# A two-layer decode step with its gradients: first MLP's products ahead of its turnings, three early zero pieces, three of K's groups loaded a second time

## The chip, the cores and the metric

The kernel is one program on one core of a Trainium2 chip. The metric is the device time of one execution in microseconds (us). The core has five engines that run beside each other and wait for each other by semaphores: TensorE (PE in the profile; its weight loads are PEld), VectorE (DVE), ScalarE (ACT), GpSimd (POOL) and SyncE (SP, which here only starts transfers). 16 DMA engines move data between the chip's memory (HBM) and the on-chip memory (SBUF); TensorE writes to PSUM, which has 8 banks.

## The reference

One token passes through attention (A), an MLP (B), the same attention and the same MLP again, with the same weights both times. Then the gradients of the output with regard to the input, both caches and all weights are returned.

```python
def _A_ref(x, k_cache, v_cache, wq, wo):          # x [1,1,1024]; caches [1,4,32768,128]
    W = min(4096, max(256, Sk // 4))              # 4096: only the last 4096 keys count
    q = (x @ wq).reshape(B, Sq, Hq, Dh)           # 32 heads of 128, 4 groups of keys
    k = jnp.repeat(k_cache[:, :, Sk - W:, :], rep, axis=1)
    v = jnp.repeat(v_cache[:, :, Sk - W:, :], rep, axis=1)
    p = _softmax(jnp.einsum("bhqd,bhkd->bhqk", q, k) * (Dh ** -0.5), axis=-1)
    return (p @ v).reshape(...) @ wo              # wo [4096,1024]
def _B_ref(x, w1, b1, w2):                        # w1 [1024,3584], w2 [3584,1024]
    h = x @ w1 + b1
    return (h * jnp.tanh(softplus(h))) @ w2
x = x + _A_ref(_layernorm(x), ...)
x = x + _B_ref(_layernorm(x), ...)
x = x + _A_ref(_layernorm(x), ...)
x = x + _B_ref(_layernorm(x), ...)
_out, _vjp = jax.vjp(_f, A_x, A_k_cache, A_v_cache, A_wq, A_wo, B_w1, B_b1, B_w2)
return (_out, *_vjp(grad_out))
```

All data are bf16. The gradients of the two caches are as large as the caches (4 x 32768 x 128 each), and zero outside the last 4096 keys: 56 MB of zeros have to be written. (MB here and below, where sizes of tiles and pieces are told, is 1024 x 1024 bytes.)

## The kernel before

**Stages in order.** Attention of layer 0, MLP of layer 0 ("first MLP"), attention and MLP of layer 1, then backward: MLP of layer 1 (its first part is done in the forward pass, below), attention of layer 1, MLP of layer 0, attention of layer 0, and at the end the outer products that make the weight and cache gradients (the "wide" stage, which takes PSUM in tiles of 1024 columns, named `wide`), evacuated to SBUF and stored. The order is written out by hand: the program has no scheduler, and each engine does its instructions in the order of the code.

**Weights and slots.** All loads go through one queue, SP's. `Ring` (the class at the top) holds a list of wanted transfers and eight slots of 1 MB; `pump` starts the next wanted transfer as soon as a slot is free, and `release` frees a slot and pumps. Its order is K, queries of layer 0, V, two chunks of w2 (`EARLY_2`), wo, w1, the other five chunks of w2 (chunk 3 goes to `zt`, the tile that later holds zeros), then three chunks of wq for layer 1 (five stay in the ring from layer 0, `KEEP_Q`), wo, wq, w2, wo and wq for what follows. A slot is freed where its last reader stands in the code, so what stands early in the code of a stage sets when the next load starts.

**Zeros.** `zeros(n, after)` (line 259 to 264) writes n pieces of 1 MB of zeros out of `zt`, by DMAs from POOL's queue; with `after`, POOL first copies one element of a tile, and so waits until that tile is computed. There are 56 such pieces. `zt` is set to zero (line 728) after the first MLP, which uses it for chunk 3 of w2.

**Products with one vector.** A product of a weight matrix with a vector uses the matrix as TensorE's stationary operand, 128 x 128 at a time, and has one moving column. The backward products need the matrix transposed: `turned` (line 446) transposes eight blocks on TensorE into a PSUM bank (line 450, the "turning"), `evac` copies them back over the matrix (line 303 on DVE, line 306 on ACT), and `mv` (line 462) does the product. `later` holds products back so that TensorE does other work while a copy runs; `flush` does all that are held back. Alternatively `rowdot` (line 427) does such a product on DVE, row by row. `rows_chunk` splits a chunk of four rows between the two.

**First MLP** (lines 716 to 738). w2 comes in seven chunks. For each, `mlp_out` (line 673) multiplies with the activation `AC` for the forward result; and since the gradient that arrives at the very end is an input, the same chunk is used at once for the backward product of layer 1's MLP, the `da` values: two rows on DVE, two turned. Chunks 0 and 1 had their `da` done earlier on DVE. `last_da` does chunk 6 as the first thing of the next stage, through `q_hook`, called once after the layer norm of layer 1's attention; it ends the collection of `da1`.

**K and V.** K is loaded in natural order into `W1S`, turned into `KT` by `kt_transposes` (line 587), and used so by the scores of both layers. V is used as it comes, in `VS`. The backward products need K in natural order and V turned, so all 32 units of eight blocks (`conv_units`, 16 of K, 16 of V) are turned in place, on TensorE (line 602) with a copy on ACT or DVE. `conv(n, eng)` does the next n units; `conv_pe` and `conv_ev` do the two halves. Units are placed where other work waits: one after the scores, one beside the softmax, one after each of eight chunks of the output projection (`wo_hook1`), eight after layer 1's MLP (line 767, beside `deriv`), and two for each chunk of the backward output projection of layer 1 (`do` hook) until none is left.

**Backward.** `dn_b1` does w1's backward product of layer 1, `ln_bwd` the layer norm's, whose hook `beside` is called twice around a small product on TensorE. `attn_bwd` has its own hooks: `do` after each of eight wo chunks, `dp`, `dq`, and `dn` after each of eight wq chunks. In layer 0 the `dn1` hook writes zero pieces at t = 3, 6 and 7, and `units_a0` (as `beside`) starts the final stage's units.

## Time and profile before

| what | value |
|---|---|
| median of 3 runs (lowest to highest) | 460.42 us (459.21 to 463.47) |
| the profiled execution's own time | 461.23 us |
| its span, first to last instruction | 459.2 us |
| TensorE / its weight loads / DVE / ACT / POOL busy | 341.7 / 276.6 / 256.6 / 225.0 / 38.7 us |
| bytes moved by DMA, mean rate | 179.38 MB, 391 GB/s (MB and GB of ten) |
| of it on SP's queue (q1), on POOL's (q0), for instructions (q8) | 119.74, 58.72, 0.80 MB |
| mean granted TensorE clock | 0.629 |

Some places in the profiled execution, in us from the start of the span: the first MLP's products start at 90.35 and its result is there at 105.45 (DVE, line 385); the queries of layer 1 are ready at 120.40; layer 1's attention result at 150.49; the gradient enters the backward attention of layer 1 at 191.31 and of layer 0 at 298.05 (DVE, line 846); the wide stage starts at 353.85 (TensorE, line 1015); the last computing instruction ends at about 437, and SP issues the last store at about 448.

How to read it: the page of the profile has the busy times, then the span in 40 slices of 11.48 us with one digit of busy share each, the granted TensorE clock and the DMA rate; then queues; then the chain of work that ended last; then groups of equal instructions by line. A line can be that of a helper (306 is every copy on ACT). The trace answers more: instructions in order of time on one engine, with the idle time before and what ended it in brackets, and the busy time of every engine in a chosen stretch (columns: length, then PE, PEld, DVE, ACT and POOL busy with counts, granted clock, DMA share, GB/s).

### The profile page before, as it was taken

What the parts mean: (1) busy time and instruction counts of PE and PEld (TensorE: products, weight loads), DVE (VectorE), ACT (ScalarE), POOL (GpSimd) and SP (SyncE); (2) the same over time, 40 slices, a digit from 0 to 9 for tenths busy, and PEclk for the clock granted to TensorE, in tenths of its full rate; (3) what the DMA queues carried; (4) which work ended last, traced back from release to release, by engine and by line L of the source; (5) the groups of instructions that cost most, each with busy time, mean ns of one, the idle gap of its engine ahead of it and who ended that gap; (6) DMA issues with size and microseconds to landing.
All of it is one profiled execution on the core that took longest, in us unless ns stands there. A gap on an engine that the chain in (4) does not pass through costs nothing. (4 is left out here: it accounts for less than half of the span.)

```text
span 459.2 us, 14200 instructions
## 1 busy us (share of the span) xinstructions
PE 341.7 (74%) x6361; PEld 276.6 (60%) x6361; DVE 256.6 (56%) x516; ACT 225.0 (49%) x261; POOL 38.7 (8%) x85
## 2 busy tenths in 40 slices
PE   3836445598679888598879798798797888889900
PEld 3735434497569887498779798697693222224600
DVE  4505731283060149677528676657456999998810
ACT  2502001055045379377317555157064999999900
POOL 1000000030103322200211000101221000000000
PEclk9955555555555569699759955589586555555555
DMA  8999999877999999999999988999999999999995
GB/s 337 421 420 418 418 419 416 361 278 261 385 425 422 421 417 418 415 399 415 420 422 418 421 320 298 347 344 368 422 419 424 412 422 422 418 421 416 405 407 213
DMA packets 27802, 179.38 MB, mean 391 GB/s; under 512 B 3642, under 2 KB 3670, under 8 KB 9430
## 3 DMA queue, kind: packets, MB, share of 16 engines
q1 hardware_dynamic: 19586, 119.74, 65.5%
q0 software_dynamic: 8064, 58.72, 30.9%
q8 instruction: 49, 0.80, 0.6%
q14 instruction: 11, 0.09, 0.0%
q10 hardware_dynamic: 92, 0.02, 0.0%
HBM read 79.74 MB, written 98.62 MB: 388 GB/s over the span
## 5 line engine op out<-in xcount | busy, mean ns | idle before, releaser
L306 ACT COPY ring<-BIG 128x1024 bf16<-128x1024 bf16 x62 | 60.7, 1014 | 41.5 <-PE BIG L450 36.1
L450 PE MATMUL BIG<-ident_bf,ring 128*128 128x128 bf16 x744 | 67.4, 255 | 1.8 <-ACT W L306 1.1
L450 PEld LDWEIGHTS <-ring 128*128 128x128 bf16 x816 | 61.5, 116 | 2.8 <-issue 2.2
L1015 PE MATMUL wide<-W 2*128 2x512 bf16 x228 | 52.1, 598 | 9.3 <-ACT W L306 2.0
L427 DVE CUSTOM_DVE_ANT_0 junk<-ring,SC 128x1024 bf16<-128x1024 bf16 x34 | 41.3, 1215 | 5.4 <-DMA ring<-in_B_w_dram 3.7
L1015 PEld LDWEIGHTS <-W 2*128 2x128 bf16 x240 | 12.6, 102 | 44.3 <-issue 43.2
L462 PEld LDWEIGHTS <-ring 128*128 128x128 bf16 x912 | 31.6, 98 | 9.3 <-ACT ring L306 6.7
L306 ACT COPY KT<-BIG 128x1024 bf16<-128x1024 bf16 x22 | 21.8, 1016 | 30.3 <-PE BIG L602 28.7
L303 DVE CAST ring<-wide 128x1024 bf16<-128x1024 f32 (+1 forms) x29 | 33.7, 1199 | 3.2 <-PE wide L1015 1.5
L306 ACT COPY W<-BIG 128x1024 bf16<-128x1024 bf16 x28 | 26.7, 1119 | 16.0 <-PE BIG L788 14.9
L306 ACT CAST ring<-wide 128x1024 bf16<-128x1024 f32 (+1 forms) x35 | 32.9, 1018 | 1.3 <-PE wide L1066 0.5
L303 DVE COPY ring<-BIG 128x1024 bf16<-128x1024 bf16 x31 | 21.3, 690 | 19.3 <-PE BIG L450 12.2
L264 POOL DMA_DIRECT2D out_dram<-zt x56 | 29.7, 534 | 22.9 <-DMA out_dram<-zt 22.0
L621 PE MATMUL MV<-NB,W 128*128 128x1 bf16 x448 | 16.2, 172 | 9.3 <-DMA W<-in_B_w_dram 6.5
L493 PE MATMUL MV<-NA,ring 128*128 128x1 bf16 x512 | 14.9, 165 | 11.0 <-DMA ring<-in_A_wq_dram 8.6
L621 PEld LDWEIGHTS <-W 128*128 128x128 bf16 x448 | 15.9, 118 | 9.8 <-DMA W<-in_B_w_dram 7.2
L303 DVE CAST VS<-wide 128x1024 bf16<-128x1024 f32 (+1 forms) x17 | 19.7, 1186 | 3.6 <-PE wide L1015 3.0
L1066 PE MATMUL wide<-W 32*128 32x256 bf16 x128 | 20.9, 402 | 0.9 <-ACT ring L306 0.8
L306 ACT CAST KT<-wide 128x1024 bf16<-128x1024 f32 x20 | 20.4, 1032 | 1.8 <-PE wide L1015 0.9
L493 PEld LDWEIGHTS <-ring 128*128 128x128 bf16 x512 | 14.2, 103 | 11.5 <-DMA ring<-in_A_wq_dram 9.1
L427 DVE CUSTOM_DVE_ANT_0 junk<-ring,DSX 128x1024 bf16<-128x1024 bf16 x16 | 19.6, 1224 | 1.1 <-DMA ring<-in_B_w_dram 0.7
L427 DVE CUSTOM_DVE_ANT_0 junk<-W,SC 128x512 bf16<-128x512 bf16 (+1 forms) x20 | 15.8, 791 | 6.5 <-PE SC L330 5.8
(268 smaller groups left out, 566.9 us busy)
## 6 DMA issues: line engine op xcount, KB each, us to landing
out_dram<-zt POOLq DMA_DIRECT2D x56, 1024.0 KB, 16.2
ring<-in_A_wq_dram SPq DMA_DIRECT2D x22, 1024.0 KB
ring<-in_A_wo_dram SPq DMA_DIRECT2D x14, 1024.0 KB
ring<-in_B_w_dram SPq DMA_DIRECT2D x13, 1024.0 KB
W<-in_A_wo_dram SPq DMA_DIRECT2D x10, 1024.0 KB
W<-in_B_w_dram SPq DMA_DIRECT2D x8, 896.0 KB
out_dram<-ring SPq DMA_DIRECT2D x7, 1024.0 KB
out_dram<-ring SPq DMA_DIRECT2D x13, 512.0 KB
```

Source lines behind the costliest of these rows:

```text
L264: nc.gpsimd.dma_start(dst, zt[:])
L303: nc.vector.tensor_copy(dst, src)
L306: nc.scalar.copy(dst, src)
L427: nc.vector.tensor_tensor_reduce(out=out, in0=a, in1=vec, scale=1.0, scalar=acc if i else 0.0, op0=ALU.mult, op1=ALU.add, accum_out=acc)
L450: nc.tensor.transpose(b[:, i * P:(i + 1) * P], block(w, i) if block else w[:, i * P:(i + 1) * P], ident_bf[:])
L462: nc.tensor.matmul(out, lhsT=w[:, i * P:(i + 1) * P], rhs=rhs_of(i), start=fresh[0], stop=last and i == n - 1, skip_group_check=True)
L493: nc.tensor.matmul(q_ps[:, h:h + 1], lhsT=ch[:, h * P:(h + 1) * P], rhs=NA[:, t, l:l + 1], start=(k == 0 and h == 0), stop=(k == TD - 1), ...
L621: nc.tensor.matmul(h_ps[:, fb:fb + 1], lhsT=f_block(W1[:, t], fb), rhs=NB[:, t, l:l + 1], start=(t == 0 and fb == 0), stop=(t == TD - 1), ...
L1015: nc.tensor.matmul(b[:, 512 * i:512 * i + 512], lhsT=R[at:at + 2, lo:lo + P], rhs=R[at:at + 2, ro + 512 * i:ro + 512 * i + 512], start=Tru ...
L1066: nc.tensor.matmul(b[:, k * 256:(k + 1) * 256], lhsT=RT[32 * g:32 * g + 32, a, tp, :], rhs=YS[32 * g:32 * g + 32, :], start=True, stop=Tru ...
```

## The change

Five edits stand in one diff.

1. First MLP: `turned` is cut into `turn_pe` and `turn_ev`, and the loop over chunks is written out. Chunk 2's turning stands first, then the forward products of chunks 0, 1, 2 and 3, with turnings, copies, DVE's rows and the products of the turned rows between and behind them. Chunks 5 and 6 are turned in the next stage: `q_hook` is now called with -1 where it was called before, and with k after each of the eight query chunks, and `last_da` does its parts at -1, 1 and 3. A chunk is released after its turned rows' products (`da_mv`).
2. Three zero pieces are written right after `zt` is set to zero; the hook `dn1` writes one piece instead of four in all.
3. `K_TURNED = 1`: only K's group 0 is turned back. Groups 1, 2 and 3 are loaded a second time from the cache into `KT`, by three transfers of 1 MB on SP's queue that stand behind the last product with `KT` in layer 1's scores. 20 units are left.
4. The 20 units stand elsewhere: one after the scores, two beside the softmax, one behind the softmax's sum, two in the output projection (chunks 2 and 5), one before the MLP's first product, four after the MLP, three and one around `ln_bwd` in `dn_b1`, five in the backward output projection (chunks 1 to 5).
5. `beside` gets the number of its call.

```diff
--- before.py
+++ after.py
@@ -402,10 +402,10 @@
         nc.vector.scalar_tensor_tensor(out=t2[:], in0=dn[:], scalar=1.0, in1=n32[:], op0=ALU.mult, op1=ALU.mult,
                                        accum_out=st[:, 1:2])
         if beside is not None:
-            beside()
+            beside(0)
         nc.tensor.matmul(TP[:, 128:130], lhsT=onesD[:], rhs=st[:], start=True, stop=True)
         if beside is not None:
-            beside()
+            beside(1)
         ab = tmp([P, 2], FP32, "ab")
         nc.vector.tensor_copy(ab[:], TP[:, 128:130])
         nc.vector.scalar_tensor_tensor(out=t2[:], in0=n32[:], scalar=ab[:, 1:2], in1=dn[:], op0=ALU.mult,
@@ -443,12 +443,19 @@
         while lag:
             lag.popleft()[1]()
 
-    def turned(w, n, mv, eng=None, block=None):
+    def turn_pe(w, n, block=None):
 
         b = big().bitcast(BF16)
         for i in range(n):
             nc.tensor.transpose(b[:, i * P:(i + 1) * P], block(w, i) if block else w[:, i * P:(i + 1) * P], ident_bf[:])
+        return b
+
+    def turn_ev(w, b, n, eng=None):
         evac(w, b[:, 0:n * P], eng, cost=(0.69 * n / 8, n / 8))
+
+    def turned(w, n, mv, eng=None, block=None):
+
+        turn_ev(w, turn_pe(w, n, block), n, eng)
         later(mv, True)
 
     fresh = [False]
@@ -484,7 +491,7 @@
         if first:
             kt_transposes()
         if q_hook is not None:
-            q_hook()
+            q_hook(-1)
         q_ps = MV[:, 0:HQ]
         order = list(range(TD)) if l == 0 else sorted(range(TD), key=lambda t: t not in KEEP_Q)
         for k, t in enumerate(order):
@@ -496,6 +503,8 @@
                 ring.keep(("q", 0, t), ("q", 1, t))
             else:
                 ring.release(("q", l, t))
+            if q_hook is not None:
+                q_hook(k)
         qv = QC[:].rearrange("p v (g u l h) -> p v g u l h", g=G, u=2, l=2)
         nc.vector.tensor_scalar(out=qv[:, 0, :, 0, l, :], in0=q_ps.rearrange("p (g h) -> p g h", g=G), scalar1=scale,
                                 scalar2=None, op0=ALU.mult)
@@ -512,6 +521,8 @@
             nc.vector.reduce_max(m64[i][:], SC[i].rearrange("p (tp c) -> p c tp", c=64), axis=AX.X)
         if not first:
             conv(1, "A")
+            for g in range(K_TURNED, G):
+                nc.sync.dma_start(KT[:, g], kv_src(A_k_cache, g))
         nc.vector.tensor_tensor(out=m64[0][:], in0=m64[0][:], in1=m64[1][:], op=ALU.max)
         m32 = small[:, 128:160]
         m64v = m64[0][:].rearrange("p (g u h) -> p g u h", g=G, u=2)
@@ -527,7 +538,7 @@
         nm = small[:, 224:288]
         nc.vector.tensor_copy(nm[:], TP[:, 192:256])
         if not first:
-            late = conv_pe(1)
+            late = conv_pe(2)
         for i in range(2):
             s = SC[i].rearrange("p (tp c) -> p tp c", c=64)
             nc.vector.tensor_tensor(out=s, in0=s, in1=nm[:, None, :].to_broadcast([P, 8, 64]), op=ALU.subtract)
@@ -550,6 +561,8 @@
         for u in range(2):
             nc.tensor.matmul(TP[:, 256:288], lhsT=onesD[:], rhs=ssv[:, :, u, :], start=(u == 0), stop=(u == 1))
 
+        if not first:
+            conv(1, "A")
         rs = small[:, 288:320]
         nc.vector.tensor_scalar(out=rs[:], in0=TP[:, 256:288], scalar1=float(D), scalar2=None, op0=ALU.mult)
         nc.vector.reciprocal(rs[:], rs[:])
@@ -588,7 +601,8 @@
                 evac(KT[:, g, 8 * b8:8 * b8 + 8, :], b.rearrange("p (t s) -> p t s", t=8))
             ring.release(("K", g))
 
-    conv_units = [(KT, g, b8) for g in range(G) for b8 in range(4)] + [(VS, g, b8) for g in range(G) for b8 in range(4)]
+    K_TURNED = 1
+    conv_units = [(KT, g, b8) for g in range(K_TURNED) for b8 in range(4)] + [(VS, g, b8) for g in range(G) for b8 in range(4)]
     conv_units.reverse()
 
     def conv_pe(n):
@@ -615,6 +629,8 @@
     def mlp_fwd(l, x, st):
         name = f"B{l}"
         n32, rstd = ln_fwd(x, st, NB[:, :, l], name)
+        if l:
+            conv(1, "A")
         h_ps = MV[:, 192:192 + TF]
         for t in range(TD):
             for fb in range(TF):
@@ -716,31 +732,76 @@
     mp0 = sB0["deriv"]()
     y_ps = MV[:, 256:256 + TD]
     mv_open()
-    for c in range(7):
+    held = {}
+
+    def da_out(c):
+        mlp_out(0, ring.get(("2", 0, c)), c, y_ps)
+
+    def da_dots(c):
         ch = ring.get(("2", 0, c))
-        mlp_out(0, ch, c, y_ps)
-        flush()
+        for tt in range(2):
+            rowdot(ch[:, tt, :], [gbc], D, da1[:, 4 * c + tt:4 * c + tt + 1])
+
+    def da_turn(c):
+        ch = ring.get(("2", 0, c))
+        held[c] = [(ch[:, tt, :], turn_pe(ch[:, tt, :], TD)) for tt in (2, 3)]
+
+    def da_put(c):
+        for w, b in held[c]:
+            turn_ev(w, b, TD, "A")
+
+    def da_mv(c):
+        for tt, (w, _) in zip((2, 3), held.pop(c)):
+            r = DA + 4 * c + tt
+            mv(w, TD, TP[:, r:r + 1], lambda i: GB[:, i, 1:2], True)
+        ring.release(("2", 0, c))
+
+    da_turn(2)
+    for c in range(3):
+        da_out(c)
         if c in EARLY_2:
             ring.release(("2", 0, c))
-        elif c < 6:
-            rows_chunk(ch, c, GB, 1, gbc, da1, DA)
-            later(lambda c=c: ring.release(("2", 0, c)))
+    da_put(2)
+    da_dots(2)
+    da_out(3)
+    da_turn(3)
+    da_put(3)
+    da_dots(3)
+    da_mv(2)
+    da_out(4)
+    da_mv(3)
     nc.gpsimd.memset(zt[:], 0.0)
+    zeros(3)
+    da_turn(4)
+    da_put(4)
+    da_dots(4)
+    da_out(5)
+    da_dots(5)
+    da_mv(4)
+    da_out(6)
     x2, st2 = residual(y_ps, x1, "B0")
 
 
-    def last_da():
-
-        rows_chunk(ring.get(("2", 0, 6)), 6, GB, 1, gbc, da1, DA)
-        flush()
-        ring.release(("2", 0, 6))
-        v = da1[:, 8:TF].rearrange("p (a b) -> p a b", b=4)[:, :, 2:4]
-        nc.vector.tensor_copy(v, TP[:, DA + 8:DA + TF].rearrange("p (a b) -> p a b", b=4)[:, :, 2:4])
+    def last_da(k):
+
+        if k == -1:
+            da_turn(5)
+            da_put(5)
+            da_dots(6)
+        elif k == 1:
+            da_mv(5)
+            da_turn(6)
+            da_put(6)
+        elif k == 3:
+            da_mv(6)
+            v = da1[:, 8:TF].rearrange("p (a b) -> p a b", b=4)[:, :, 2:4]
+            nc.vector.tensor_copy(v, TP[:, DA + 8:DA + TF].rearrange("p (a b) -> p a b", b=4)[:, :, 2:4])
 
     def wo_hook1(c):
         if c == 0:
             zeros(7, OC[:, 0, 1:2])
-        conv(1)
+        if c in (2, 5):
+            conv(1)
 
     DR = {}
     stg = DSX[0:2 * HQ, 1024:1024 + 4 * P].rearrange("p (k i) -> p k i", k=4)
@@ -764,7 +825,7 @@
     zeros(8, x3)
     sB1 = mlp_fwd(1, x3, st3)
     put_by("NB", NB, TD)
-    conv(8, "A")
+    conv(4, "A")
     mp1 = sB1["deriv"]()
 
 
@@ -800,7 +861,8 @@
                 turned(w, n, lambda w=w, f0=f0, n=n, t=t, k=k: mv(w, n, TP[:, t:t + 1], lambda i: DHC[:, f0 + i, 1:2], k == 1),
                        "A", f_block)
         flush()
-        return ln_bwd(dnp, sB1["n32"], sB1["rstd"], g, "B1")
+        conv(3, "A")
+        return ln_bwd(dnp, sB1["n32"], sB1["rstd"], g, "B1", lambda k: conv(k, "A"))
 
     def rowize_f():
 
@@ -952,7 +1014,7 @@
             zeros(1, dnp[:, t:t + 1])
 
     g2 = attn_bwd(1, sA1, g3, ("o", 1), ("q", 2), KEEP_Q2,
-                  dict(do=lambda c: conv(2), dp=dp3, dq=dq3, dn=dn3))
+                  dict(do=lambda c: conv(1 if 1 <= c <= 5 else 0), dp=dp3, dq=dq3, dn=dn3))
 
 
     ROWS = W1S[:, 0:5120]
@@ -1142,14 +1204,14 @@
         zeros(4, DQC[:, 0, 0:1])
 
     def dn1(t):
-        if t in (3, 6, 7):
-            zeros(2 if t == 3 else 1, dnp[:, t:t + 1])
+        if t == 3:
+            zeros(1, dnp[:, t:t + 1])
         if t == 4:
             twins()
         if t == 5:
             todo[0].append(units_cols(0, 8, out_4))
 
-    def units_a0():
+    def units_a0(k):
 
         even()
         load["D"] += 10
```

## The prediction

> **What bounds the kernel now.** I read the page's slices first, then the DMA queues, then stretches around the two dips, and last POOL's own order of work. The slices:
>
> ```profile
> DMA  8999999877999999999999988999999999999995
> GB/s 337 421 420 418 418 419 416 361 278 261 385 425 422 421 417 418 415 399 415 420 422 418 421 320 298 347 344 368 422 419 424 412 422 422 418 421 416 405 407 213
> ```
>
> Transfers run at 415 to 425 GB/s almost everywhere. Only two stretches fall short: about 80 to 126 us (first MLP and the queries of layer 1) and 264 to 321 us. The stretches show why, and what the end looks like:
>
> ```profile
> 91.84:103.32 11.48, 11.11 (x245) 10.87 (x243) 9.93 (x17) 5.78 (x6) 3.51 (x1) 0.50 0.74 278
> ...
> 436.24:447.72 11.48, 0.75 (x4) 0.19 (x2) 2.01 (x2) 1.09 (x2) 0.00 (x0) 0.50 1.02 407
> 447.72:459.20 11.48, 0.00 (x0) 0.00 (x0) 0.00 (x0) 0.00 (x0) 0.00 (x0) 0.50 0.53 213
> ```
>
> In the dip TensorE is busy 11.11 of 11.48 us and DMA 0.74: weights wait for ring slots. After 437 us nobody computes and DMA works off stores for 20 us. So the end is the end of a queue of transfers; arithmetic matters only if it leaves that queue empty. The chain of waits, which follows engines, is silent about this.
>
> The 16 DMA engines are not equal. Each transfer leaves 16 completion marks; by these the zero pieces (1024 KB each; I call that a piece) of 145 to 208 us finish on the fastest engine every 2.46 us and on the slowest every 2.71. POOL shows the slow pace in its own rows, since each issue waits for a piece issued eight before:
>
> ```profile
> 172.53 0.53 POOL L264 DMA_DIRECT2D out_dram<-zt x1 [2.12 <-DMA out_dram<-zt]
> 175.21 0.53 POOL L264 DMA_DIRECT2D out_dram<-zt x1 [2.15 <-DMA out_dram<-zt]
> 177.92 0.53 POOL L264 DMA_DIRECT2D out_dram<-zt x1 [2.18 <-DMA out_dram<-zt]
> 180.67 0.53 POOL L264 DMA_DIRECT2D out_dram<-zt x1 [2.22 <-DMA out_dram<-zt]
> ```
>
> Every transfer is complete only when the slowest engine has done its sixteenth, so that engine is the bound. Its marks: third query load at 116.23, the zero piece of g2 at 277.16; between them landed 21 loads and 40 zero pieces, 61 pieces in 160.93 us, 2.64 us each. Last zero piece 361.99, last store about 458, 38 pieces of stores: 2.53 each.
>
> **Parts of the change: transfers.** K's reload adds three pieces at about 130 us, where DMA is full: 3 x 2.64 = +7.9 us (2.46 to 2.71 each: 7.4 to 8.1). The three early zero pieces add no bytes; three fewer remain in the last query stage. What pays is idle time of the slowest engine that gets filled:
> - First dip: from 107.84 (first query load landed) to 116.23 only two pieces land; at 2.5 to 2.64 each that leaves 3.1 to 3.4 us idle. memset is free at 99.7 us as now (below), 3.51 us long, issue at 103.3; before, a first zero piece moved 3.5 to 5 us after its issue, so data flows from 107. Nearly all of this idle time is filled. The idle time before 107 stays.
> - Second dip: 277.16 to 332.02 lands 19 pieces in 54.9 us; at 2.5 to 2.64 each, 4.7 to 7.4 us idle. The six added or advanced pieces, and any time that arithmetic gains, arrive here as queued zeros, so I count it as filled but for 0.5.
>
> Sum: +7.9, minus 3.1 to 3.4, minus 4.2 to 6.9, plus 0.3 for the first loads coming later: between -2.1 and +0.9. I take -0.5, the middle.
>
> The Trainium skill, page "DMA: Bandwidth & Descriptors", section "Specifications", puts a core's HBM limit near 358 GB/s; by that three pieces (3.15 MB) would take an estimated 8.8 us and the sum would move up by 0.9. This trace's 415 to 425 GB/s contradict the limit.
>
> **First MLP.** Its loop now:
>
> ```profile
> 90.35 2.70 PE L673 MATMUL MV<-AC,ring 128*128 128x1 bf16 x96 [2.41 <-DVE AC L648]
> 92.91 1.87 PE L450 MATMUL BIG<-ident_bf,ring 128*128 128x128 bf16 x16
> 94.57 1.04 PE L673 MATMUL MV<-AC,zt 128*128 128x1 bf16 x32
> 95.47 0.84 PE L462 MATMUL TP<-GB,ring 128*128 128x1 bf16 x16
> ```
>
> By starts: products of a chunk 0.90, turning two rows 1.66, their products 0.70. The change puts chunk 2's turning ahead of everything. Chunk 2's last mark is at 90.53, AC is ready at 90.29: turning ends 92.2, and chunks 0 and 1 give back their slots 1.85 us later. Chunk 4's load follows at 93.2 (now 91.37) and lands at 98.2 (now 96.31); chunk 2 is released at 98.2 (now 96.40); chunk 6 lands near 104.2 (now 102.51). With out6 x2 comes at 105.2, now 105.45: turnings left the loop, but the loads set the end. Then turning 5 fits the layer norm; turnings 5 and 6 and their products among the queries cost 0.70 + 1.66 + 0.70. The third query load is issued earlier (109.7, now 111.14) but shares DMA with zeros: with half the rate from 110.5 it lands near 122, so queries are ready at 122.9, now 120.40: **+2.5 us**. Bounds: 0 (zeros later than thought) to +4.
>
> **Turnings taken from K.** Of 32 units 12 vanish (8 transposes and a copy each). By place: the output-projection loop has two units instead of eight; a unit there moves the next product by 0.80:
>
> ```profile
> 138.00 1.01 PE L602 MATMUL BIG<-ident_bf,KT 128*128 128x128 bf16 x8
> 138.80 1.04 PE L573 MATMUL MV<-OC,ring 128*128 128x1 bf16 x32
> ```
>
> That is -4.8, of which some 2 go back, since the eighth projection weight now lands near 149 (marks now 141 to 144). With 0.3 for the extra units beside the softmax (1.01 each, mostly under DVE's 129.65 to 131) and 0.9 gained where no unit stands before the layer norm, the chain is at -1.2. After the second MLP four units instead of eight: DVE's row products start at 170.59, four units earlier about 166.2: cumulative -4.4. Three units after dn_b1's last products lie under DVE (TensorE is done 186.7, DVE 189.2): +0.3; if TensorE stays at half clock longer, up to +2. In the backward output loop five units instead of fourteen; two take 0.88 at full clock, 1.51 at half: 1.5 + 5 x 0.44 + 0.9 = -4.7. Bound: the same loop of layer 0, without units, takes 22.9 us (298.05 to 320.97) against 29.85 (191.31 to 221.16), so at most -6.9; none if DVE or loads hold it. The chain reaches DOC at **-8.8 us**.
>
> From there it gives this back. SP waits for a landing eight transfers back, and K's three stand in that order, but they land by 165, long before the next loads. Yet zeros queue: at 197 about ten pieces, now near none by 213. Loads beside zeros move 0.20 of 0.40 MB per us (now 255 to 261 us), some 5.2 us a piece. Query weights of dn3 still come in time (last near 239, needed 248). Second MLP chunks 5 and 6 come 1 to 2 us late, the last four projection weights of layer 0 at 304, 309, 314, 318: the stage ends near 321, as now. The wide stage starts at 354 to 357 (now 353.85), and zeros are worked off near 361.5, so stores wait for nothing. Cover left: 5 us.
>
> **Rivals.** *A, forecast:* bytes traded for idle time, 459.2 - 0.5 = 458.7 span; the execution took 461.23, 2.0 more, and the median of the runs is 460.42; taking 0.5 from the median gives **460**. Own range 457 to 464. Chance 0.58.
>
> *B, the slowest engine does not bind* and the mean rate counts: 170 pieces less the 39 landed by 107.84, plus three, are 134; at the full slices' 0.397 a us, 338 us, with the tail of 5.7 us after the bulk ends (453.5): 451.5 to 452.5, so 453 to 454 by the median. For it: 15 engines do pieces in 2.46, and arithmetic runs 8.8 us ahead. Against: POOL's 2.7 us rows. Chance 0.22.
>
> *C, slower:* late loads make the wide stage late, not just the loads. Place: second MLP and the projection of layer 0. It decides once the wide stage starts after 361.5, when zeros are gone and DMA stands still. Without the 8.8 gained, 4.9 queued pieces (six less 1.1 absorbed in the first dip) delay loads by 4.9 x 2.64 = 13 us: start 366.8, 5.3 us idle, plus 0.5 of uncertain sum: 466. For it: loads already end waits there; TensorE's unexplained stalls ("issue", up to 2.3 us) all lie where DMA is full, and the second dip would be full:
>
> ```profile
> 276.68 1.22 DVE L427 CUSTOM_DVE_ANT_0 junk<-ring,SC 128x1024 bf16<-128x1024 bf16 x1 [3.31 <-DMA ring<-in_B_w_dram]
> ```
>
> Against: a full DMA is never idle while it delays. Chance 0.20.
>
> **Numbers.** Range 454 to 466: A's range, most of C, the upper part of B. One per cent, 4.6 us, is about what a measurement of this kernel can tell from no change: faster by more 0.22, within 0.58, slower by more 0.20.
>
> **What would show it.** Slices 80 to 126 and 264 to 321 at about 415 GB/s; x2 near 105, queries near 123, DOC of layer 1 near 213; zeros ending near 361 with three fewer after 344; a wide start of 354 to 357. Wrong if the slices stay low in the second dip, if the wide stage starts after 361, or if stores finish with no straggling engine.

## The result, and the profile after

| | before | changed |
|---|---|---|
| device time, median of 20 runs (lowest to highest) | 460.2 us (459.21 to 463.47) | 463.48 us (461.39 to 465.76) |
| profiled execution: device time, span | 461.23, 459.2 us | 465.04, 463.26 us |
| bytes moved | 179.38 MB | 182.53 MB |
| x2 / queries of layer 1 / end of its projection | 105.45 / 120.40 / 150.49 us | 105.39 / 124.53 / 154.90 us |
| DOC of layer 1 / end of attention backward, layer 1 | 222.14 / 261.79 us | 220.89 / 260.98 us |
| dh of layer 0 / DOC of layer 0 / start of the wide stage | 288.43 / 321.88 / 353.85 us | 291.84 / 326.64 / 361.30 us |

The changed kernel takes 1.0066 times as long as the one before, 95% interval 1.0053 to 1.0080. That is 0.7% slower: within the 1% that the prediction called no change, but on the other side of it, and measurable over so many runs. The slices of the page after:

```profile
DMA  8999999779999999999999999959998699999997
GB/s 336 424 419 417 422 417 419 329 274 332 423 423 422 424 418 426 423 406 424 423 423 422 422 422 427 372 222 396 419 424 362 241 416 412 419 419 413 409 406 312
```

The first dip is still there. The second has shrunk to two slices (290 to 313 us), and there is a third, which was not there before: 362 and 241 GB/s at 347 to 371 us. To weigh them I divided both traces into the same stretches; the last two columns are the DMA share and the rate. Before:

```profile
80.00:130.00 50.00, 35.80 (x900) 33.97 (x901) 20.11 (x59) 13.92 (x17) 4.92 (x4) 0.50 0.86 329
130.00:255.00 125.00, 106.44 (x2224) 101.13 (x2222) 66.33 (x166) 71.08 (x82) 21.41 (x45) 0.73 1.01 417
255.00:342.00 87.00, 74.72 (x1609) 69.60 (x1607) 54.09 (x119) 40.89 (x47) 7.77 (x18) 0.69 0.96 365
342.00:372.00 30.00, 24.54 (x270) 10.26 (x267) 25.46 (x37) 23.81 (x32) 2.64 (x7) 0.59 1.01 418
```

The changed kernel:

```profile
80.00:130.00 50.00, 34.65 (x891) 33.01 (x891) 19.04 (x55) 13.67 (x17) 6.44 (x7) 0.50 0.87 345
130.00:255.00 125.00, 101.42 (x2133) 95.76 (x2133) 65.44 (x165) 65.55 (x76) 20.67 (x43) 0.72 1.01 421
255.00:342.00 87.00, 70.32 (x1503) 65.13 (x1501) 49.52 (x112) 36.51 (x42) 8.53 (x21) 0.65 0.95 386
342.00:372.00 30.00, 23.11 (x346) 13.38 (x345) 21.72 (x36) 20.16 (x27) 0.70 (x2) 0.67 0.80 328
```

Taking 422 GB/s for full, the rate of the full slices, a stretch is short of full by its length times (422 - rate) / 422. So the change filled 1.9 us in the first dip, 1.2 in the middle and 4.3 in the second dip, opened 6.4 us of new idle time at 342 to 372 us, and lost 0.3 at 372 to 420 (417 GB/s there, 420 before). The 3.15 MB more take 7.5 us at that rate. That makes +6.8; the span grew by 4.1, so the tail after 420 us must hold 2.7 us less idle time. It does: 13.75 MB in 39.2 us before, 16.56 MB in 43.26 us now, which at the same rate leaves 6.6 and 4.0 us idle. In the new idle stretch DMA stands nearly still around the start of the wide stage; the stretch 354 to 364 us of the changed kernel (before, the same stretch has 415 GB/s):

```profile
354.00:364.00 10.00, 5.76 (x31) 1.70 (x32) 3.56 (x13) 6.28 (x12) 0.00 (x0) 0.50 0.37 153
```

The first instruction of the wide stage on TensorE, and SP's first store of that stage, in order of time, changed kernel:

```profile
361.30 1.05 PE L1077 MATMUL wide<-W 2*128 2x512 bf16 x7 [0.80 <-ACT W L322]
...
362.98 0.82 SPq L1056 DMA_DIRECT2D out_dram<-VS  x2
```

The zeros were worked off at 360.2 us (last mark of the slowest engine; the fast ones were done near 358), and nothing was there to store.

### The profile page after: what moved, and what is told of

Its sections match the earlier page's. It is cut to its first block, busy times and chain, and to the rows that moved or that the text cites. A ratio compares the mean times of both kernels' runs of the same rounds, so it can differ in the third digit from the quotient of the medians.

```text
span 463.3 us, 13997 instructions
## 1 busy us (share of the span) xinstructions
PE 335.5 (72%) x6265; PEld 270.0 (58%) x6265; DVE 253.6 (55%) x511; ACT 218.3 (47%) x254; POOL 38.3 (8%) x83
## 2 busy tenths in 40 slices
DMA packets 28234, 182.53 MB, mean 394 GB/s; under 512 B 3690, under 2 KB 3718, under 8 KB 9478
## 5 line engine op out<-in xcount | busy, mean ns | idle before, releaser
L450 PE MATMUL BIG<-ident_bf,ring 128*128 128x128 bf16 x744 | 68.8, 258 | 4.7 <-DMA ring<-in_B_w_dram 2.9
L450 PEld LDWEIGHTS <-ring 128*128 128x128 bf16 x816 | 62.3, 117 | 5.5 <-DMA ring<-in_B_w_dram 3.0
L427 DVE CUSTOM_DVE_ANT_0 junk<-ring,SC 128x1024 bf16<-128x1024 bf16 x34 | 41.3, 1216 | 10.7 <-DMA ring<-in_B_w_dram 9.2
L469 PEld LDWEIGHTS <-ring 128*128 128x128 bf16 x912 | 32.0, 99 | 12.2 <-issue 8.2
L500 PEld LDWEIGHTS <-ring 128*128 128x128 bf16 x512 | 14.9, 104 | 15.3 <-DMA ring<-in_A_wq_dram 13.2
L306 ACT COPY KT<-BIG 128x1024 bf16<-128x1024 bf16 x10 | 9.8, 1010 | 18.4 <-PE BIG L616 16.9
L306 ACT COPY VS<-BIG 128x1024 bf16<-128x1024 bf16 x13 | 12.7, 1016 | 12.3 <-PE BIG L616 12.3
```

The lines of the kernel that those rows point to most:

```text
L306: nc.scalar.copy(dst, src)
L427: nc.vector.tensor_tensor_reduce(out=out, in0=a, in1=vec, scale=1.0, scalar=acc if i else 0.0, op0=ALU.mult, op1=ALU.add, accum_out=acc)
L450: nc.tensor.transpose(b[:, i * P:(i + 1) * P], block(w, i) if block else w[:, i * P:(i + 1) * P], ident_bf[:])
L469: nc.tensor.matmul(out, lhsT=w[:, i * P:(i + 1) * P], rhs=rhs_of(i), start=fresh[0], stop=last and i == n - 1, skip_group_check=True)
L500: nc.tensor.matmul(q_ps[:, h:h + 1], lhsT=ch[:, h * P:(h + 1) * P], rhs=NA[:, t, l:l + 1], start=(k == 0 and h == 0), stop=(k == TD - 1), ...
```

## The experiments

I held three theories. **Theory 1**: too many pieces stand in front of weight loads (and of TensorE's own code), the chain of arithmetic arrives late at the wide stage, and DMA runs dry ahead of it. **Theory 2**: only bytes and filled idle time count, as in the forecast. **Theory 3**: the first MLP's new order costs the time. Ratios are against the kernel before on the same chip, with 95% intervals; "rest" is the span less the start of the wide stage.

| run | device time | ratio | wide start | rest |
|---|---|---|---|---|
| before (beside e1 to e4) | 459.99 | | 353.85 | 105.35 |
| changed | 463.48 | 1.0066 [1.0053, 1.0080] | 361.30 | 101.96 |
| e1 changed, no early zeros | 462.91 | 1.0066 [1.0044, 1.0088] | 353.89 | 106.73 |
| e2 early zeros alone | 461.04 | 1.0017 [0.9999, 1.0035] | 358.86 | 101.56 |
| e3 K alone | 462.00 | 1.0037 [1.0021, 1.0054] | 354.24 | 106.04 |
| e4 first MLP alone | 459.86 | 0.9995 [0.9978, 1.0012] | 353.55 | 104.03 |
| e5 before, without zeros | 445.67 | one run | 342.39 | 101.50 |
| e6 changed, without zeros | 440.54 | one run | 336.97 | 101.66 |
| e7 changed, one early zero | 461.10 | 1.0018 [1.0000, 1.0035] | 354.18 | 105.30 |
| e8 K alone, no second load | 458.65 | 0.9970 [0.9950, 0.9990] | 352.66 | 104.06 |
| e9 before, first MLP, one early zero | 459.18 | 0.9987 [0.9973, 1.0000] | 353.22 | 102.79 |
| e10 changed, three zeros fewer in the middle | 463.87 | 1.0079 [1.0063, 1.0096] | 357.69 | 104.55 |
| e11 e9 and one zero more at g2 | 460.86 | 0.9999 [0.9977, 1.0021] | 356.97 | 101.57 |
| e12 changed, reload later | 463.25 | 1.0077 [1.0058, 1.0097] | 358.61 | 102.13 |
| e13 changed, two early zeros | 461.21 | 1.0032 [1.0014, 1.0049] | 356.29 | 102.37 |
| e14 changed, again | 463.96 | 1.0090 [1.0066, 1.0114] | 357.98 | 102.12 |

### The three parts, one by one

e1 takes the early zeros out of the changed kernel:

```diff
-    zeros(3)
     da_turn(4)
...
-        if t == 3:
-            zeros(1, dnp[:, t:t + 1])
+        if t in (3, 6, 7):
+            zeros(2 if t == 3 else 1, dnp[:, t:t + 1])
```

> The changed kernel with its three early zero pieces put back into the last query stage; the first MLP's new order and K's reload stay. Theory 1 (too many pieces are queued in the middle, so weight loads and TensorE's own code arrive late and the wide stage starts late): three pieces fewer stand before the second MLP, the wide stage starts at about 356 instead of 361.3, the device time is 460 to 461. Theory 2 (DMA is bound by its bytes, the engines' idle time decides): the first dip is idle by another 3 us, 464 to 466. Theory 3 (the new order of the first MLP is what costs): no change, 463 to 464.

e2 is the kernel before with these zeros moved, and nothing else:

```diff
     nc.gpsimd.memset(zt[:], 0.0)
+    zeros(3)
...
-        if t in (3, 6, 7):
-            zeros(2 if t == 3 else 1, dnp[:, t:t + 1])
+        if t == 3:
+            zeros(1, dnp[:, t:t + 1])
```

> The kernel before with nothing but three zero pieces moved from the last query stage to the point behind the first MLP's memset. Theory 1: queries of layer 1 about 2 to 4 us late and the pieces stay queued up to the second MLP, 461 to 463. Theory 2: 3 us of idle DMA time filled at no price, 457 to 458. Theory 3: no change, 460.

e3 is the kernel before with K's part of the change only; the other places of `conv` are those of the change, too:

```diff
+            for g in range(K_TURNED, G):
+                nc.sync.dma_start(KT[:, g], kv_src(A_k_cache, g))
...
+    K_TURNED = 1
-    conv_units = [(KT, g, b8) for g in range(G) for b8 in range(4)] + ...
+    conv_units = [(KT, g, b8) for g in range(K_TURNED) for b8 in range(4)] + ...
...
-        conv(1)
+        if c in (2, 5):
+            conv(1)
...
-                  dict(do=lambda c: conv(2), dp=dp3, dq=dq3, dn=dn3))
+                  dict(do=lambda c: conv(1 if 1 <= c <= 5 else 0), dp=dp3, dq=dq3, dn=dn3))
```

> The kernel before with nothing but K's three groups loaded again and the remaining turnings at their new places; first MLP and zeros as before. Theory 1: layer 1 loses turnings but gets loads and code late, the wide stage starts 2 to 5 us later than 353.85, 461 to 463. Theory 2: three pieces more at 2.64 us less the 4 to 7 us of idle time in the second dip, 461 to 464, with the wide stage no later than before. Theory 3: no change or a gain, 457 to 460.

e4 is the kernel before with the new first MLP and `last_da(k)` only, which against the changed kernel is:

```diff
-    zeros(3)
     da_turn(4)
...
-                nc.sync.dma_start(KT[:, g], kv_src(A_k_cache, g))
...
-    K_TURNED = 1
+    K_TURNED = G
```

(and `conv` and the zeros of `dn1` at the places of before)

> The kernel before with nothing but the first MLP's new order (products ahead of turnings, turnings 5 and 6 among the queries); zeros, K and its turnings as before. Theory 1: x2 within 0.3 us of before, queries at 120 to 121, 459.5 to 460.5. Theory 2: the same bytes and the same idle time, 460. Theory 3: the turning of chunk 2 ahead of the products and the turnings among the queries cost 2 to 4 us, 462 to 464.

Measured: first MLP nothing (-0.05%), the early zeros +0.17%, K +0.37%; together they would make +0.49%, the whole is +0.66%. On the kernel before, **theory 3 falls**. Beside K it is less clear: e1 is e3 with the new first MLP, and it lies 0.29%, some 1.3 us, above e3; its time, 462.91 us, is nearest to theory 3's 463 to 464. The two intervals overlap, so a price of about 1 us for the first MLP beside K is neither shown nor excluded. e3 came as theory 2 had it (no later wide start, 461 to 464 us). But theory 2 falls with e2, which was to gain 3 us. Its stretches show why; e2 at 80 to 130 and at 342 to 372 us:

```profile
80.00:130.00 50.00, 35.84 (x899) 33.90 (x900) 19.96 (x59) 13.91 (x17) 6.44 (x7) 0.50 0.90 357
...
342.00:372.00 30.00, 25.31 (x354) 14.10 (x353) 23.90 (x38) 22.38 (x29) 0.71 (x2) 0.67 0.75 301
```

By the sum above the three pieces fill 3.3 us of the first dip (357 against 329) and leave 8.3 us idle at 342 to 372 (301 against 418). What is filled early is gone later. e1 brought the wide start back to 353.89, but not the time: theory 1 had 460 to 461. Without early zeros the chain is in time, and bytes set the end. So the changed kernel can lose its time in two ways that cost about the same: DMA has too much to move (e1), or the chain is late (changed).

### Chain and code without the zeros

```diff
-    zjobs.reverse()
+    zjobs.clear()
```

> The kernel before without any of its 56 zero pieces (that part of two outputs is left unwritten), so that its weight loads and TensorE's code find DMA free; its time is read only for the pace of the chain. Theory 1 (the pauses of TensorE that no semaphore ends are waits of its code behind a full DMA, and loads wait behind zeros): these pauses fall from 10.7 us in sum to under 2; DOC of layer 1, 222.1 with zeros, comes at 205 to 213. Rival (the pauses belong to the matmuls, the loads to their slots): the pauses stay near 10 us and DOC comes at 218 to 222.

> The changed kernel without any of its 56 zero pieces, to be read beside the kernel before without them. Theory 1: the pauses fall from 18.9 us to under 2, and what the change takes from the arithmetic up to DOC of layer 1 is seen bare: DOC 8 to 11 us earlier than before without zeros (8.8 was forecast). Rival (the arithmetic had no such gain): DOC within 3 us of before without zeros.

DOC of layer 1 came at 217.53 (e5) and 208.54 us (e6): **9.0 us earlier by the change, 8.8 forecast.** The start of the wide stage in e5 and e6:

```profile
342.39 1.04 PE L1015 MATMUL wide<-W 2*128 2x512 bf16 x7 [0.80 <-ACT W L322]
```

```profile
336.97 1.04 PE L1077 MATMUL wide<-W 2*128 2x512 bf16 x7 [0.80 <-ACT W L322]
```

The changed kernel's arithmetic is thus 5.4 us faster up to the wide stage, and with zeros it is 7.45 us slower (4.1 in e14, the same kernel in another execution): the zeros delay the chain before by 11.5 us and the changed one by 24.3 (21.0 in e14). From the wide start on, both take about 101.6 us (101.50, 101.66). That gives a rule for this kernel, which every row of the table follows: **the span is at least about wide start + 101.6 us; where pieces are left over at that moment, it is longer.** The changed kernel (101.96), e2, e11, e12, e13 and e14 (up to 102.4) stand on the rule's floor: the chain binds. Before, e1, e3 and e7 (105.3 to 106.7) have 3.7 to 5.1 us of pieces left over: the bytes bind. e4, e8, e9 and e10 lie between.

TensorE's pauses that no semaphore ends fell to 4.9 us (from 10.7) and 8.4 us (from 18.9), not under 2 as expected: the larger ones that stay lie behind loads that alone fill DMA (119 to 125 us in both, 145 and 215 us in e6). Between 150 and 190 us, where DMA is nearly free without zeros, there are none; e1 and e3 have one of 1.7 and 1.8 us at 157, but before and the changed kernel have none there either. What they are is told below.

### How many early pieces

e7 and e13 have one and two early pieces; the others go back to the last query stage. The edit of e7; e13 has `zeros(2)`, and one piece each at t = 3 and 6:

```diff
-    zeros(3)
+    zeros(1)
     da_turn(4)
...
-        if t == 3:
-            zeros(1, dnp[:, t:t + 1])
+        if t in (3, 6):
+            zeros(2 if t == 3 else 1, dnp[:, t:t + 1])
```

> The changed kernel with one zero piece at the first MLP instead of three; the other two are in the last query stage, at the fourth and seventh weight. Theory 1 (each piece queued before layer 1's weights delays the chain by one piece, and what it fills early comes back as idle time before the wide stage once that starts after the zeros are done): wide start at 356 to 357 (353.9 with none, 361.3 with three), no idle time before the first stores, 460.5 to 462. Theory 2 (only filled bytes count): 1 us below the kernel with none, about 462 at most, falling on with each piece. Rival (the three are without influence): 463.

> The changed kernel with two early zero pieces instead of three; the third is in the last query stage, at the seventh weight. The runs so far obey one rule: the span is the later of two ends, wide start plus 101.6 us (what the stores take when no zeros are left, from the two kernels without zeros), and the end of the bytes. Theory 1 (a piece delays the chain by one piece once it reaches layer 1's weights): wide start at 356.5 to 358.5, span 458.5 to 460, device time 460.5 to 462. Theory 1' (a step: from the second piece on layer 1's weights lose their places): wide start at 360 to 361.5, 462.5 to 463.5. Rival (the profiled execution of the changed kernel was an outlier, pieces do little): wide start near 354, 460 to 461.

e14 is the changed kernel once more:

> The changed kernel itself, profiled and timed again. Theory 1: wide start again after 358, DMA idle for 3 to 7 us ahead of the stores, span within 1 us of wide start plus 101.6; 463 to 464. Rival (the idle time belonged to one execution): wide start before 356.5, no idle time ahead of the stores, and the lost time stands elsewhere.

With none, one, two and three pieces the wide stage starts at 353.9, 354.2, 356.3 and 358.0 or 361.3, and the ratios are 1.0066, 1.0018, 1.0032 and 1.0066 (1.0090 in the second measurement). By the ratios (the runs stand on different chips) the first piece gains 2.2 us, the second costs 0.6, which the intervals do not tell from nothing, and the third 1.6 to 2.7. Against none, all three together gain nothing. Theory 1 had the first piece, too, delay the wide start by 2 to 3 us; it did not. The first dip tells why only one is free. e1, no early zeros, 104 to 120 us:

```profile
104.00:108.00 4.00, 3.18 (x53) 3.03 (x51) 1.86 (x12) 1.95 (x3) 0.42 (x1) 0.50 0.70 227
108.00:112.00 4.00, 3.48 (x95) 3.40 (x93) 2.35 (x4) 2.60 (x5) 0.00 (x0) 0.50 0.54 166
112.00:116.00 4.00, 4.00 (x136) 4.00 (x135) 0.17 (x1) 1.89 (x2) 0.00 (x0) 0.50 1.01 428
116.00:120.00 4.00, 2.33 (x85) 2.27 (x83) 0.00 (x0) 0.00 (x0) 0.00 (x0) 0.50 1.01 418
```

The changed kernel:

```profile
108.00:112.00 4.00, 3.48 (x94) 3.40 (x92) 2.29 (x4) 2.60 (x5) 0.00 (x0) 0.50 1.00 389
112.00:116.00 4.00, 3.69 (x122) 3.63 (x120) 0.17 (x1) 1.82 (x2) 0.00 (x0) 0.50 1.01 420
```

The zeros' data moves from 108 us on, and from 112 us DMA is full of layer 1's weights anyway: what is idle between is 2.4 us, (422 - 166) / 422 of four, one piece. The second and third run beside the weights and move them: from 114 to 120 us the trace's DMA records have 1.25 MB of zeros (queue q0) and 1.28 MB of loads (q1). (The Trainium skill, page "DMA: Bandwidth & Descriptors", section "Queues, rings and completion order", says that each DMA engine goes round its queues in turn; these equal shares agree.) The third query load and layer 1's last projection weight come late by that; TensorE's wait for the weight, changed kernel:

```profile
153.85 1.01 PE L586 MATMUL MV<-OC,ring 128*128 128x1 bf16 x32 [3.97 <-DMA ring<-in_A_wo_dram]
```

In e14 the late wide start came back, at 357.98 instead of 361.30, with the same idle stretch:

```profile
342.00:372.00 30.00, 23.90 (x330) 12.17 (x328) 23.77 (x37) 22.26 (x29) 0.70 (x2) 0.64 0.81 329
```

That execution took 461.87 us, the first 465.04: 3.2 us between the times, 3.3 between the wide starts. So these two executions of the changed kernel differ by when the wide stage starts, and a place on the chain read from one of them alone is sure to some 3 us only.

### K's second load without its bytes

e8 is e3 without the three loads, so that the products behind them use the wrong K and only the time can be read:

```diff
-            for g in range(K_TURNED, G):
-                nc.sync.dma_start(KT[:, g], kv_src(A_k_cache, g))
```

> The kernel before with K's turnings taken away as in the run with K alone, but the second load of the three groups left out (so later products use the wrong K): the turnings' part without the bytes. Theory 1: DOC of layer 1 at 205 to 212; three pieces less, of which the second dip, idle for longer, gives back 3 to 6 us: 456 to 460. Theory 2 (bytes alone, all 7.9 us of them): 454. Rival (the reload costs nothing, the moved turnings do): 462, as with the reload.

458.65 us, a ratio of 0.9970 against 1.0037 for e3: 3.1 us less. So the bytes cost 3.1 us of their 7.5; without them the second dip stays open. e8 and then e3 at 255 to 342 us:

```profile
255.00:342.00 87.00, 72.18 (x1568) 67.11 (x1565) 51.52 (x109) 38.43 (x44) 8.32 (x19) 0.66 0.94 372
```

```profile
255.00:342.00 87.00, 69.15 (x1480) 64.06 (x1476) 48.57 (x104) 37.18 (x43) 8.84 (x21) 0.66 0.98 402
```

6.2 us of the bytes fill this dip. The turnings saved, free of any price in bytes, gain 0.3% only: DOC of layer 1 at 211.37 us is 10.8 us early, the wide stage 1.2.

### Where the pieces stand

e10 takes three pieces out of the middle of the changed kernel, e12 issues the reload later:

```diff
-    zeros(8, dh1)
+    zeros(5, dh1)
...
-        if t == 3:
-            zeros(1, dnp[:, t:t + 1])
+        if t in (3, 6, 7):
+            zeros(2 if t == 3 else 1, dnp[:, t:t + 1])
```

> The changed kernel with its three early zero pieces, but three of the eight pieces issued after the second MLP forward (at dh1) moved back to the last query stage: the early place is the same, the backlog behind it is not. Theory 1a (what delays is the backlog of pieces through the backward stages of layer 1): queries and end of the projection as in the changed kernel (124.5, 154.9), then the chain recovers, DOC of layer 1 at 213 to 217, wide start at 354 to 358, 460.5 to 462. Theory 1b (the early place itself, that is layer 1's late queries and projection weights, is carried to the end): DOC at 219 to 221, wide start at 360 to 361, and three pieces more after that leave no idle time: 462.5 to 464.

```diff
-            for g in range(K_TURNED, G):
-                nc.sync.dma_start(KT[:, g], kv_src(A_k_cache, g))
...
     put_by("NB", NB, TD)
+    for g in range(K_TURNED, G):
+        nc.sync.dma_start(KT[:, g], kv_src(A_k_cache, g))
     conv(4, "A")
```

> The changed kernel with K's three second loads issued after the second MLP's NB was written (about 160 us) instead of inside the scores of layer 1 (128 to 134 us), behind layer 1's last projection weights. Theory 1c (the reload stands in front of these weights and makes them late): end of the projection at 149 to 151 instead of 154.9, wide start 2 to 5 us earlier, 461 to 462.5. Theory 1d (three zeros alone make them late): end of the projection within 1 us of 154.9, 463 to 464.

e10's chain does what theory 1a said (DOC of layer 1 at 216.48, wide start 357.69), its time what 1b said, 463.87. Against e14 (218.79 and 357.98) the gain is 2.3 us at DOC and 0.3 at the wide start, so a recovery of the wide start is not shown. e1 tells more: it has as many pieces queued before the last query stage as e10, with the three at dh1 instead of early, and its DOC is 3.5 us earlier, its wide start 3.8. So the early place itself carries most of the delay, whatever stands behind it. The stretches of e10 show where its time went:

```profile
255.00:342.00 87.00, 70.26 (x1517) 65.03 (x1516) 50.87 (x113) 37.05 (x44) 7.79 (x18) 0.67 0.92 365
342.00:372.00 30.00, 21.60 (x267) 9.83 (x266) 22.05 (x35) 20.53 (x29) 2.64 (x7) 0.60 1.01 418
```

The idle time ahead of the stores is gone (418), and the second dip is back where it was before the change (365): the same idle time at another place. e12's projection ended at 154.78 us, so the early zeros alone make its weights late (1d), as e2 had it without any reload (153.42). DOC came 5.0 us earlier than in the changed kernel, at 215.89, the wide stage 2.7 (against e14: 2.9 earlier and 0.6 later), and the time did not move.

### A version that might beat both

e9 is the first MLP's new order and one early zero on the kernel before; e11 moves one more piece to g2 and is shown against e9:

```diff
-    zeros(1, g2)
+    zeros(2, g2)
...
-        if t in (3, 6):
-            zeros(2 if t == 3 else 1, dnp[:, t:t + 1])
+        if t == 3:
+            zeros(2, dnp[:, t:t + 1])
```

> The kernel before with the first MLP's new order and one early zero piece (taken from the seventh weight of the last query stage); K and its turnings as before. Theory 1: one piece fills 1 to 2.6 us of the first dip, the wide stage starts within 1.5 us of before (353.85), so DMA is not idle before the stores for more than 1 us: 458 to 459.5, the best of all. Theory 2 (filled bytes count in full): 457.2 to 457.5. Rival (any early piece delays layer 1 as three did): wide start at 356 to 357, 460.5 to 461.

> The kernel before with the first MLP's new order, one early zero piece, and one more moved from the last query stage to the start of the second MLP of layer 0 (at g2), where DMA is at 300 to 350 GB/s. Theory 1: it fills 1 to 2.5 us there but makes the second MLP's loads late, wide start 354 to 356, zeros done before it: within 1 us of the kernel with the early piece alone, 458 to 460. Theory 2 (filled bytes count in full): 2.5 us below the kernel with the early piece alone, 455.5 to 457.

e9 has the lowest time of all complete kernels, 459.18 us, but its interval reaches 1.0000: 0.1% is at the edge of what can be told. In e11 the piece moved delayed the wide start by 3.75 us, to 356.97, which is the rule's floor again (rest 101.57). At 460.86 us it came as neither theory had it (458 to 460, 455.5 to 457): the delay was larger than theory 1 allowed.

## Why the prediction was wrong, point by point

**The failed step** is the gain put on the three early zeros: "Nearly all of this idle time is filled" and, of the other idle time, "The six added or advanced pieces ... arrive here as queued zeros, so I count it as filled". The 3.1 to 3.4 us of the first dip were a little more than one piece, and three were issued. One was free; the other two ran beside layer 1's weights and made them late, the wide stage came late, and the idle time came back at 342 to 372 us. The forecast had the eighth projection weight land "near 149"; TensorE waited for it until 153.85. The whole term was -3.1 to -3.4; e2 measured it at +0.8 (0.0 to +1.6) on the kernel before, and the changed kernel against e1 at 0 (+1.1 in e14). Without the term the forecast of -0.5 would have been +2.6 to +2.9; the ratio measured, 1.0066, is +3.0. How the second piece makes the wide stage late stays open: in e13 the projection is 1.7 us later than in e1, DOC of layer 1 is not later, and DOC of layer 0 is (323.40 against 319.22).

**The step after it** fell with it: "zeros are worked off near 361.5, so stores wait for nothing. Cover left: 5 us." The zeros were done at 360.2, the wide stage started at 361.3 (358.0 in e14) instead of 354 to 357. And the cover was wrong even so: an end that the bytes set stands beside wide start + 101.6. An estimate from e1's span, 460.6, less the 2 us that early pieces fill puts the bytes' end at 458.6, so the chain binds from a wide start of 357.0 on, not 361.5.

**The slowest DMA engine** still sets the pace of the pieces; POOL's rows of the changed kernel stand 2.7 us apart, as before:

```profile
177.86 0.53 POOL L264 DMA_DIRECT2D out_dram<-zt x1 [2.03 <-DMA out_dram<-zt]
180.55 0.53 POOL L264 DMA_DIRECT2D out_dram<-zt x1 [2.16 <-DMA out_dram<-zt]
183.26 0.53 POOL L264 DMA_DIRECT2D out_dram<-zt x1 [2.19 <-DMA out_dram<-zt]
```

**K's reload**, +7.9 less 4.2 to 6.9 in the second dip, plus 0.3, was right: that alone gives +1.3 to +4.0; e3 measured +0.37%, 1.7 us, and e1, K with the first MLP, +0.66%, 3.0 us. By the sum above the second dip filled by 7.6 us in e3 and 7.2 in e1, a little more than forecast.

**The arithmetic** behind the projection was right: the forecast has -7.6 from there to DOC, and the runs show -7.5 (e3), -7.7 (e1) and -7.8 (e6 against e5). At DOC itself -8.8 agrees with -9.0 without zeros, -9.2 in e1 and -9.6 in e3 in part by luck: the forecast's -1.2 at the end of the projection holds, by its own sum, the +2.5 for late queries, and in these runs the queries are within 0.4 us of their time before. Without that term, the others kept, it would be -3.7, and they show -1.2, -1.4 and -2.1. (Two sums slip on the way: the terms named for the projection, with the +2.5, add up to -0.9, and 1.5 + 5 x 0.44 + 0.9 is 4.6, not 4.7.) In the changed kernel the gain shows only as -1.25 at DOC, since the projection ended 4.4 us late and the backward output loop took 30.3 us against 26.65 in e1 (28.1 in e14). The loop of the changed kernel, then that of e1; the last three columns are granted clock, DMA share and rate:

```profile
190.55:220.89 30.34, 25.86 (x469) 25.34 (x470) 17.12 (x31) 17.85 (x19) 3.89 (x8) 0.80 1.01 417
```

```profile
186.33:212.98 26.65, 22.57 (x469) 21.70 (x470) 17.12 (x31) 17.36 (x19) 3.35 (x7) 0.94 1.01 412
```

Both loops have two pauses of TensorE, 3.0 and 2.5 us in sum. The difference is time in which TensorE is busy, 25.9 against 22.6 us, at a lower granted clock; why the clock was lower is not shown. In the changed kernel it was so at:

```profile
206.00:210.00 4.00, 4.00 (x68) 4.00 (x66) 2.83 (x5) 2.88 (x4) 0.03 (x1) 0.57 1.02 426
210.00:214.00 4.00, 2.32 (x43) 2.25 (x41) 0.74 (x2) 1.62 (x2) 0.50 (x1) 0.86 1.00 418
214.00:218.00 4.00, 4.00 (x80) 4.00 (x79) 3.09 (x5) 2.69 (x3) 0.00 (x0) 0.71 1.02 428
```

**That the gain is given back later** was right as well: e3 is 9.6 us ahead at DOC of layer 1, 6.3 at the end of layer 0's MLP, 1.9 at DOC of layer 0 (319.95; "the stage ends near 321"), and 0.4 us behind at the wide start. With zeros queued all along, the second MLP's loads were later than forecast ("1 to 2 us"); DVE's rows of the changed kernel:

```profile
276.86 1.22 DVE L427 CUSTOM_DVE_ANT_0 junk<-ring,SC 128x1024 bf16<-128x1024 bf16 x1 [4.31 <-DMA ring<-in_B_w_dram]
...
281.75 1.22 DVE L427 CUSTOM_DVE_ANT_0 junk<-ring,SC 128x1024 bf16<-128x1024 bf16 x1 [2.39 <-DMA ring<-in_B_w_dram]
...
286.71 1.22 DVE L427 CUSTOM_DVE_ANT_0 junk<-ring,SC 128x1024 bf16<-128x1024 bf16 x1 [2.47 <-DMA ring<-in_B_w_dram]
```

**The first MLP** was right as far as e4 shows: chunk 2's turning first, x2 at 105.39 (105.2 forecast), nothing gained, nothing lost.

```profile
90.59 1.89 PE L450 MATMUL BIG<-ident_bf,ring 128*128 128x128 bf16 x16 [2.91 <-DMA ring<-in_B_w_dram]
92.27 2.74 PE L689 MATMUL MV<-AC,ring 128*128 128x1 bf16 x96
```

**The queries** came at 124.53, 4.1 us late, against +2.5 with bounds of 0 to +4: just outside.

**The rivals.** B, the slowest engine does not bind, did not come; its "15 engines do pieces in 2.46" reads the fastest of the 16 marks only, the middle ones are 2.52 to 2.54 us apart. C did come by its mechanism, a late wide stage with DMA idle ahead of it, and in part at its place: between the end of attention backward of layer 1 and the end of the second MLP the changed kernel fell back by 5.6 us against before, in the projection of layer 0 by nothing, and behind it by 2.7 more. It was wrong in its point of decision (361.5 for some 357) and in its objection, "a full DMA is never idle while it delays": true in the moment of the delay, but the idle time follows once the queued pieces run out.

What stays open is why single executions of the changed kernel spread over 4.4 us; two traces only tie the spread to the wide start.

## What to carry to other kernels

In this kernel an idle place in the transfers took one piece of 1 MB, as much as fitted before the next needed load; what was put there beyond that delayed the loads, and the idle time returned where the pieces were missing. Keep two ends apart and price a change against both: the bytes' end, and the start of the last stage plus that stage's own length, which a run with the filler left out measures directly. Saved arithmetic that was paid with bytes gained nothing where the end was set by bytes: the saving was 9 us at one point of the chain, and a third of a per cent at the end even with the bytes given away.

## What the runs showed of the hardware

TensorE's "issue" pauses, which I could not explain before, are by two signs waits for its own code. In the 16 executions traced here all 159 pauses over 0.3 us stand at the same place of a block: after 95 matmuls counted modulo 128, each of which has its weight load, so every 256 instructions. Each ends 1.21 to 1.60 us after one of the 49 16-KB transfers of the instruction queue (q8) has ended; for instance, a packet of the changed kernel ends at 145.0 us, and the trace has

```profile
146.54 1.28 PE L586 MATMUL MV<-OC,ring 128*128 128x1 bf16 x43 [2.27 <-issue]
```

The Trainium skill, page "Runtime: NRT & Kernel Launch", section "Instruction fetch mechanics", says that code comes in blocks of 16 KiB, 256 instructions, and that crossing a block's border is "mostly hidden". The size agrees with this trace, the hiding does not, where DMA is full: the pauses add up to 10.7 us before, 18.9 in the profiled execution of the changed kernel (12.4 in e14), 20.6 in e3, and 4.9 in the kernel before without zeros. One of them stands in the last stretch ahead of the wide stage, in front of the seven last products of the query stage: 3.38 us in the changed kernel, 2.17 in e14; the last one of before, at another place of that stage, has 0.86.

```profile
355.85 0.35 PE L469 MATMUL TP<-DQC,ring 128*128 128x1 bf16 x7 [3.38 <-issue]
```

That a kernel with fewer turnings has longer pauses fits a TensorE that goes through its code faster while DMA stays full, but no run here separates the two, and not all show it: e12 (12.0) and e14 have no more than e4 (12.1), which has all the turnings.
